# Chunk selection over 576 queries at once, with 28 products of a blank tile first and all engine lists made anew

## The chip, the cores and the metric

One Trainium2 chip, of which one core is used. The metric is device time in microseconds (us). The kernel before took 272.13 us, the median of 3 runs (272.02 to 273.0).

## The reference

Attention over 4 batches of 8 heads (768 queries and keys, 64 wide), in which each query attends to 6 chunks of 32 keys, followed by a two-layer network with an ELU between the layers. Cut to what matters:

```python
ub = np.sum(np.maximum(q[..., None, :] * k_min[...], q[..., None, :] * k_max[...]), axis=-1)
ub = np.where(causal, ub, -1e9)                    # 24 chunk bounds for each query
top_chunks = np.argsort(ub, axis=-1)[..., -6:]
scores = scale * np.matmul(q, k.transpose(0, 1, 3, 2))
mask = sel & (pos[:, None] >= pos[None, :])        # sel: the key's chunk is among top_chunks
attn = softmax(np.where(mask, scores, -1e9))
x = np.matmul(attn, v)                             # to (3072 tokens, 512)
h = x @ w_in                                       # 512 -> 2048
g = np.where(h > 0, h, np.exp(np.minimum(h, 0)) - 1)
out = g @ w_out                                    # 2048 -> 512
```

## The kernel before

**Units.** Two heads make a pair, two pairs a quad; a batch has 4 pairs and 2 quads. Queries are worked in two halves of 384 (`hf` 0 and 1). Queries below 192 (`SEL0`) have at most 6 chunks ahead of them and need no choice, so the choice covers 192 queries of the first half and 384 of the second: 576 in all.

**Preparation.** Batch 0 (`SPLIT`, pairs 0 to 3) is prepared by halves in `first_prep`: rows of k and q are loaded (L666, from SP's queue, and the first four q loads from ACT's), turned on PE by fp32 transposes, six to a tile (`turn`, L689), copied out by ACT (L699 keys, L721 queries, L725 their positive part `qa`) and reduced to chunk minima and maxima on DVE (L708, L715, tile `km`). POOL casts queries into `rhs` (L741) and values into `vext` (L732). Batches 1 to 3 (`pair_prep`) are loaded in 32 x 32 pieces (L595) and turned on DVE (L607, L625), with L611, L618, L628 and L641 as the matching steps.

**The choice.** `quad_sel(g, hf)` is called for each quad and half. On PE, 16 fp32 products (L771) make the bounds of both pairs: `km` against `qt` and `qa`, each 32 columns of output by `n/2` queries (96 for the first half, 192 for the second), in a PSUM tile of class `S2`. The profile has 32 rows for them, and 32 weight loads. DVE transposes the bounds to `ubt` (L788), writes the causal entries (L793), takes the eight largest of each group of queries to `thr` (L800, one instruction for 32 queries of each of four partition groups), compares with the sixth (L805, `selv`) and transposes back (L811, `selt`). POOL copies the result into rows 64 to 87 of `rhs` (L822, four copies a call). The scores (L863) then add the mask inside the product: `lhs` carries the chunk pattern in the same rows (L535).

**Attention.** `pair_attend(u, hf)`: scores on PE (L863, in batch 0 with the causal triangle by L869), exponentials on ACT (L890, `pt`), the triangle of batches 1 to 3 by POOL (L909), products with v (L922, `psO`), division on DVE (L935, L938), transposes on PE (L947), copies on ACT (L950, `xT`).

**The network.** `mlp(b, hf)`: `up` (L972, four products of 384 columns to a tile), the ELU on ACT (L982, L987) and DVE (L990, L1011, L1016; L1000 and L1005 in the last batch), `down` (L1032, four products of 512 columns to a part), ACT's copy to `osb` (L1041) and the store (L1046). The weights are loaded by POOL's queue (L563, L567). Work of the network of one batch fills PE while the next batch is prepared and chosen.

**Order.** Every step is an `Op` with an engine, a duration, what it reads and writes, and which buffers it takes and frees. `QUEUE` holds, for each engine, the written-out list of its steps by number; `Plan.order` walks through the five lists with the durations and a model of the loads (`ALONE`, `SHARE`, `PAUSE`) to settle in which order the program is written and which buffer each step gets. On the chip each engine then runs its own list in order and waits on semaphores. `caps` says how many buffers each class has; `kept` are tiles that are set up once (`c_kept`, `c_ones`, `c_zero`, `c_rows`).

Of the kernel before, what the change touches and what calls it, by code (L numbers as in the profile page):

```python
# [13 lines left out]
F32 = mybir.dt.float32  # L14
# [4 lines left out]
S = 768  # L19
# [7 lines left out]
P = 128  # L27
# [22 lines left out]

EARLY = (4, 0)
QUEUE = {
    "DVE": [
# [21 lines left out]
    ],  # L75
    "POOL": [
# [12 lines left out]
    ],  # L89
    "ACT": [  # L90
# [20 lines left out]
    ],  # L111
# [5 lines left out]
    ],  # L117
# [43 lines left out]
class Plan:  # L161
# [71 lines left out]
    SHARE = {128: 1.0, 256: 0.35, 512: 0.3, 768: 0.3, 1024: 0.3, 2048: 0.5}  # L233
    HEAVY = 0.088
    RAMP = 240.0
    PAUSE = ((15.8,16.6),(21.9,22.7),(29.8,30.8))
    LANDED = 0.75

    def served(self, rings, t, until):
# [875 lines left out]
```

## Time and profile before

| | before |
|---|---|
| median of 3 runs | 272.13 us |
| profiled execution | 271.44 us |
| its span, first to last instruction | 269.6 us |
| PE busy | 260.3 us (97%) |
| DVE busy | 207.2 us (77%) |
| ACT busy | 200.6 us (74%) |
| POOL busy | 122.3 us (45%) |
| bounds on PE (L771), instructions | 512 matmul rows in 16 calls |

An engine's share is of the whole span. In a timeline a row has its start, its duration, the engine, line and tiles, and in brackets how long the engine stood idle before it and what ended that. Matmuls overlap, so durations of rows on PE add up to more than PE's time; the distance from start to start is what a step costs.

### The profile page before, as it was taken

Reading aid. Unit: us, or ns where it says so; the run is one execution under the profiler, and the core shown is the slowest. Engines: PE = TensorE matmul, PEld = TensorE weight load, DVE = VectorE, ACT = ScalarE, POOL = GpSimd, SP = SyncE. Lnnn points to the kernel's source line nnn. Section 1 sums busy time; section 2 is a strip of 40 time slices with the busy share of each in tenths; the row PEclk is TensorE's granted clock in tenths of the full one; section 3 lists DMA queues with packets and bytes.
Section 4 is the critical chain, followed back from the end, with each engine's and each line's share of the span. In section 5 each row is a group of like instructions: output and inputs, shape, how many; then the busy total and the mean of one; then the engine's idle time right before and its main releaser. Section 6 shows DMA issues by size and latency. Waiting matters only on the chain.

```text
span 269.6 us, 7062 instructions
## 1 busy us (share of the span) xinstructions
PE 260.3 (97%) x2648; PEld 162.8 (60%) x2648; DVE 207.2 (77%) x562; ACT 200.6 (74%) x375; POOL 122.3 (45%) x233
## 2 busy tenths in 40 slices
PE   4998899999999999999999999999999999999995
PEld 3986566655566655655655566565666555654544
DVE  5789899899999999999898946686666785444440
ACT  4899899757996989998999386986888843234322
POOL 3697971175995798745871167434610000000000
PEclk9999999999999999999999999999999999999999
DMA  7998999989996998999621020000030100102103
GB/s 222 268 233 118 203 215 213 182 165 163 186 174 106 191 212 152 165 180 221 127 80 41 0 80 0 2 2 1 2 117 4 39 0 24 58 2 78 72 6 119
DMA packets 112626, 29.82 MB, mean 111 GB/s; under 512 B 101200, under 2 KB 109648, under 8 KB 112592
## 3 DMA queue, kind: packets, MB, share of 16 engines
q1 hardware_dynamic: 107280, 24.39, 46.0%
q0 software_dynamic: 4224, 4.19, 9.4%
q10 hardware_dynamic: 1088, 0.79, 0.9%
q8 instruction: 21, 0.34, 0.6%
q14 instruction: 13, 0.11, 0.1%
HBM read 27.26 MB, written 6.29 MB: 124 GB/s over the span
## 4 chain that ended last, share of the span: by engine, by line
PE 90%; ACT 5%; DVE 2%; DMA 1%; issue 1%; POOL 0%; ACTq 0%
PE psH L972 23%; PE psM L1032 23%; PE psS L863 13%; PE psO L922 8%; PE psS L972 8%; PE psMT L1032 8%; PE psS L771 3%; ACT lhs L699 2%; ACT pt L890 2%; PE psT L947 2%; DMA gT<-in_k_dram 1%; PE psMT L689 1%; PE psH L689 1%; PE psS L869 1%; ACT qa L725 0%
## 5 line engine op out<-in xcount | busy, mean ns | idle before, releaser
L890 ACT ACTIVATE pt<-psS 128x768 bf16<-128x768 f32 (+2 forms) x120 | 89.9, 777 | 7.7 <-PE psO L922 4.0
L972 PE MATMUL psH<-xT,w_in_sb 128*128 128x384 bf16 x384 | 75.0, 326 | 0.0
L1032 PE MATMUL psM<-w_out_sb,gT 128*128 128x512 bf16 x288 | 71.8, 379 | 0.0
L972 PEld LDWEIGHTS <-w_in_sb 128*128 128x128 bf16 x512 | 47.8, 97 | 33.0 <-issue 1.2
L1032 PEld LDWEIGHTS <-gT 128*128 128x128 bf16 x400 | 37.4, 97 | 33.6
L982 ACT ACTIVATE f<-psH 128x384 f32<-128x384 f32 x96 | 48.1, 505 | 10.8 <-PE psH L972 8.8
L863 PE MATMUL psS<-rhs,lhs 88*128 88x384 bf16 (+4 forms) x304 | 54.5, 283 | 0.7 <-ACT pt L890 0.5
L909 POOL TENSOR_SCALAR_AFFINE_SELECT pt<-pt 128x512 bf16<-128x512 bf16 (+1 forms) x48 | 24.6, 521 | 48.3 <-ACT pt L890 47.6
L1011 DVE SCALAR_TENSOR_TENSOR t<-f,psH 128x384 bf16<-128x384 f32 x56 | 30.2, 544 | 10.8 <-ACT f L982 10.0
L822 POOL COPY rhs<-selt 24x192 bf16<-24x192 bf16 (+1 forms) x64 | 27.2, 424 | 22.2 <-DVE selt L811 19.6
L863 PEld LDWEIGHTS <-lhs 88*128 88x128 bf16 x304 | 27.6, 97 | 14.6 <-ACT pt L890 1.5
L741 POOL CAST rhs<-f 64x768 bf16<-64x768 f32 (+1 forms) x40 | 28.2, 706 | 13.4 <-DVE f L625 6.5
L1016 DVE SCALAR_TENSOR_TENSOR gT<-psH,t 128x384 bf16<-128x384 f32 x56 | 30.5, 549 | 1.0
L922 PEld LDWEIGHTS <-pt 128*128 128x128 bf16 x672 | 27.2, 98 | 6.0 <-ACT pt L890 0.6
L922 PE MATMUL psO<-vext,pt 128*128 128x65 bf16 x672 | 29.7, 194 | 0.3 <-ACT pt L890 0.2
L741 POOL CAST lhs<-f 64x768 bf16<-64x768 f32 x24 | 19.7, 821 | 12.1 <-DVE f L607 11.1
L982 ACT ACTIVATE f<-psS 128x768 f32<-128x768 f32 x16 | 12.9, 811 | 16.5 <-PE psS L972 16.4
L990 DVE SCALAR_TENSOR_TENSOR gT<-f,psH 128x384 bf16<-128x384 f32 x40 | 21.6, 543 | 3.6 <-ACT psH L987 3.1
L972 PE MATMUL psS<-xT,w_in_sb 128*128 128x384 bf16 x128 | 22.9, 326 | 0.0
L1000 DVE TENSOR_SCALAR t<-f 128x768 bf16<-128x768 f32 x16 | 8.9, 558 | 17.5 <-ACT f L982 17.5
L1032 PE MATMUL psMT<-w_out_sb,gT 128*128 128x512 bf16 (+1 forms) x112 | 22.1, 349 | 0.0
L950 ACT ACTIVATE xT<-psT 128x384 bf16<-128x384 bf16 x32 | 15.4, 498 | 8.4 <-PE psT L947 8.3
(55 smaller groups left out, 299.3 us busy)
## 6 DMA issues: line engine op xcount, KB each, us to landing
out_dram<-osb SPq DMA_DIRECT2D x23, 256.0 KB, 2.3
f<-in_k_dram SPq DMA_DIRECT2D x48, 96.0 KB, 4.1
f<-in_q_dram SPq DMA_DIRECT2D x48, 96.0 KB, 3.5
f<-in_v_dram SPq DMA_DIRECT2D x24, 192.0 KB, 3.8
w_in_sb<-in_moe_w_in_dram POOLq DMA_DIRECT2D x4, 512.0 KB, 8.0
w_out_sb<-in_moe_w_out_dram POOLq DMA_DIRECT2D x4, 512.0 KB, 12.4
gT<-in_k_dram SPq DMA_DIRECT2D x8, 192.0 KB, 4.0
gT<-in_v_dram SPq DMA_DIRECT2D x12, 128.0 KB, 4.3
```

Source lines behind the costliest of these rows:

```text
L741: nc.gpsimd.tensor_copy(out=o, in_=i)
L822: eng.tensor_copy(out=dst.rearrange("c h (i two x) -> c h i two x", two=2, x=32)[:, :, :, odd, :], in_=tiles[st][r0:r0 + NCH, c0:c0 + n].r ...
L863: nc.tensor.matmul(p_s[:, hd, pc:pc + w], lhsT=tiles[pt_["kb"]][0:64 + NCH, hd, 128 * kb:128 * kb + 128], rhs=tiles[pt_["qb"]][0:64 + NCH, ...
L890: lambda bs=bs, pt=pt, wtot=wtot, lo=lo, at=at: nc.scalar.activation(out=tiles[pt][:, :, lo:lo + wtot], in_=tiles[bs[0]][:, :, at:at + wto ...
L909: nc.gpsimd.affine_select(out=a, in_=a, compare_op=AOT.is_ge, fill=0.0, base=0, pattern=pat, channel_multiplier=-1)
L922: nc.tensor.matmul(po[:, hd, qi, :], lhsT=tiles[pt][:, hd, off:off + 128], rhs=tiles[pt_["vx"]][:, 6 * hd + kb, :], start=(kb == 0), stop= ...
L972: nc.tensor.matmul(ph, lhsT=w_in_sb[:, kk, f0:f0 + 128], rhs=tiles[XT[4 * b + kk]][:, c0:c0 + HALF], start=(kk == 0), stop=(kk == NKK - 1))
L982: lambda e=e, view=view: nc.scalar.activation(out=halves(e)[:, 0:step], in_=view(), func=AF.Exp),
L990: lambda e=e, view=view, fc=fc, gt=gt: nc.vector.scalar_tensor_tensor(out=tiles[gt][:, fc:fc + step, :], in0=halves(e)[:, 0:step], scalar= ...
L1011: lambda e=e, t=t, view=view: nc.vector.scalar_tensor_tensor(out=tiles[t][:, 0:step], in0=halves(e)[:, 0:step], scalar=1.0, in1=view(), op ...
L1016: lambda t=t, view=view, fc=fc, gt=gt: nc.vector.scalar_tensor_tensor(out=tiles[gt][:, fc:fc + step, :], in0=view(), scalar=0.0, in1=tiles ...
L1032: nc.tensor.matmul(pm, lhsT=tiles[gt][:, fc, 128 * tt:128 * tt + 128], rhs=w_out_sb[:, fc, x0:x1], start=(fc == 0), stop=(fc == NFC - 1))
```

## The change

`quad_sel` gains a form for the whole row of queries: for batches 1 to 3 it is called once for each quad, with `hf=None`, and works on all 576 queries (288 columns to a product, 18 groups on DVE, transposes of 576, POOL copies of 24 x 576). Batch 0 keeps its halves. The tiles `ubt`, `thr` and `selv` grow from 12 to 18 groups, and `ubt` and `thr` have one buffer where they had two. Each call now frees the query tiles `qt` and `qa` that it read.

PE's list starts with `c_warm`: 28 bf16 products of 128 columns of a tile `blank`, which DVE fills with zeros as its first step. The result is not read.

The lists of all engines are new, with new numbers of the planner: `ALONE` 0.0188 and 0.0368 for 256 and 768 bytes, four `PAUSE` intervals, no `late` for the first loads, and other durations for the bounds on PE. Among what moves: DVE fills `ident_f` behind the five fills of `rhs`, and the copies of L535 partly behind the first reductions; POOL makes `trineg` behind the first casts; on SP the first six loads of v (L671) go ahead of the second half of k and q, of which one k load stood ahead of them.

```diff
+WARM = 28
 QUEUE = {            # all five lists replaced
...
-    ALONE = {128: 0.0138, 256: 0.0194, 512: 0.036, 768: 0.038, 1024: 0.055, 2048: 0.085}
+    ALONE = {128: 0.0138, 256: 0.0188, 512: 0.036, 768: 0.0368, 1024: 0.055, 2048: 0.085}
-    PAUSE = ((15.8,16.6),(21.9,22.7),(29.8,30.8))
+    PAUSE = ((0.0, 2.28), (17.2, 17.8), (21.6, 22.4), (30.5, 31.3))
...
-            "ubt": 2, "thr": 2, "selv": 2, "selt": 2, "pt": 10, "t": 3, "gT": 3,
+            "ubt": 1, "thr": 1, "selv": 2, "selt": 2, "pt": 10, "t": 3, "gT": 3,
...
+    blank = const.tile([P, P], BF16, name="blank")
-        "selv": [const.tile([P, 12, 32], BF16, ...
+        "selv": [const.tile([P, 18, 32], BF16, ...
-        "kx": ([P, NCH], F32), "ubt": ([P, 12, 32], F32), "thr": ([P, 12, 8], F32),
+        "kx": ([P, NCH], F32), "ubt": ([P, 18, 32], F32), "thr": ([P, 18, 8], F32),
...
+    add("DVE", 0.12, -10.5, lambda: nc.vector.memset(blank, 0.0), writes=["blank"])
     add("DVE", 0.5, -9.9, c_fill, writes=["fill"])
+    bw, = new("S2")
+
+    def c_warm():
+        for i in range(WARM):
+            nc.tensor.matmul(tiles[bw][:, 0, 0:128], lhsT=blank, rhs=blank, start=True, stop=True)
+    add("PE", 0.107 / 2 * WARM, -1000.0, c_warm, reads=["blank"], alloc=[bw], free=[bw])
...
     def quad_sel(g, hf):
         pairs = (2 * g, 2 * g + 1)
+        whole = hf is None
+        hs = (0, 1) if whole else (hf,)
+        end = whole or hf == 1
+        hf = 0 if whole else hf
...
-            n = HALF - SEL0 if hf == 0 else HALF
+            n = S - SEL0 if whole else HALF - SEL0 if hf == 0 else HALF
...
-                if hf or u in SPLIT:
-                    fr += [PAIR[u]["qt", hf], PAIR[u]["qa", hf]]
-                if hf:
+                fr += [PAIR[u]["qt", hf], PAIR[u]["qa", hf]]
+                if end:
                     fr += [PAIR[u]["km"]]
-            add("PE", 0.0025 * n + 0.073, pr, ub, reads=rd, writes=[bu[0]], alloc=bu, free=fr)
+            add("PE", 0.00167 * n + 0.27, pr, ub, reads=rd, writes=[bu[0]], alloc=bu, free=fr)
...
-                        reads=[(st, hf)], writes=[(qb, hf, odd, "left")], ...
+                        reads=[(st, x) for x in hs], writes=[(qb, x, odd, "left") for x in hs], ...
...
             for g in (2 * b, 2 * b + 1):
-                for hf in range(2):
-                    quad_sel(g, hf)
+                quad_sel(g, None)
```

More of the change, by code (lines that the diff above doesn't have):

```diff
@@ L53 @@
     "DVE": [
[21 rows of a table removed]
[20 rows of a table added]
+    ],
[32 rows of a table added]
     ],
     "POOL": [
[12 rows of a table removed]
[10 rows of a table added]
     ],
     "ACT": [
[20 rows of a table removed]
[20 rows of a table added]
     ],
     "SP": [
[4 rows of a table removed]
-    ],
[32 rows of a table removed]
[4 rows of a table added]
     ],
@@ L444 @@
         "km": [const.tile([P, 2, 32], F32, name=f"km{i}") for i in range(caps["km"])],
-        "selv": [const.tile([P, 12, 32], BF16, name=f"selv{i}") for i in range(caps["selv"])],
+        "selv": [const.tile([P, 18, 32], BF16, name=f"selv{i}") for i in range(caps["selv"])],
     }
@@ L571, in weights, with fetch @@
         add("DMA", 0.0, -20.0, lambda: None, reads=[("asked", i)], writes=[name], lat=plan.LANDED)
-    def fetch(starts, packets, size, pr, f, writes, eng="SP", more=(), late=0.0, **kw):
+    def fetch(starts, packets, size, pr, f, writes, eng="SP", more=(), **kw):
         uid[0] += 1
@@ L577, in fetch @@
         add(eng, 0.533 * starts, pr, f, reads=more, writes=[w] + writes, lat=0.0,
-            move=(0 if eng == "SP" else 1, (1.08 if eng == "SP" else 1.3) + late, 0.533, starts, packets, size), **kw)
+            move=(0 if eng == "SP" else 1, 1.08 if eng == "SP" else 1.3, 0.533, starts, packets, size), **kw)
         add("DMA", 0.0, pr, lambda: None, reads=[w], writes=writes, lat=plan.LANDED)
@@ L674, in first_prep @@
         early = u - SPLIT[0] < EARLY[hf]
-        late = 0.35 if u == SPLIT[0] and hf == 0 else 0.0
-        fetch(1, 256, 768, pl, load(i0, kr), [(sg, i0)], late=late, alloc=[sg] if u == SPLIT[0] else [])
+        fetch(1, 256, 768, pl, load(i0, kr), [(sg, i0)], alloc=[sg] if u == SPLIT[0] else [])
         fetch(1, 256, 768, (pl + 0.1) - 300.0 * early, load(i0 + 1, qr, nc.scalar if early else nc.sync), [(sg, i0 + 1)],
-              eng="ACT" if early else "SP", late=late)
+              eng="ACT" if early else "SP")
         if u % 2 == 0:
@@ L776, in quad_sel @@
             for u in pairs:
-                rd += [PAIR[u]["qt", hf], PAIR[u]["qa", hf], (PAIR[u]["km"], 0, hf), (PAIR[u]["km"], 1, hf)]
-                if hf or u in SPLIT:
-                    fr += [PAIR[u]["qt", hf], PAIR[u]["qa", hf]]
-                if hf:
+                rd += [PAIR[u]["qt", hf], PAIR[u]["qa", hf]] + [(PAIR[u]["km"], i, x) for i in range(2) for x in hs]
+                fr += [PAIR[u]["qt", hf], PAIR[u]["qa", hf]]
+                if end:
                     fr += [PAIR[u]["km"]]
-            add("PE", 0.0025 * n + 0.073, pr, ub, reads=rd, writes=[bu[0]], alloc=bu, free=fr)
+            add("PE", 0.00167 * n + 0.27, pr, ub, reads=rd, writes=[bu[0]], alloc=bu, free=fr)
             ut, = new("ubt")
@@ L812, in t2 @@
                                     in_=tiles[sv].rearrange("p a b -> p (a b)")[:, 0:n])
-            add("DVE", dve(n), pr, t2, reads=[sv], writes=[(st, hf)], alloc=[] if hf else [st], free=[sv])
+            add("DVE", dve(n), pr, t2, reads=[sv], writes=[(st, x) for x in hs], alloc=[] if hf else [st], free=[sv])
             for j, u in enumerate(pairs):
@@ L826, in quad_sel @@
                     add("DVE" if fast else "POOL", 0.075 + 0.00027 * n if fast else 0.20 + 0.00095 * n, pr + 0.01, put,
-                        reads=[(st, hf)], writes=[(qb, hf, odd, "left")], free=[st] if hf and j and odd else [],
+                        reads=[(st, x) for x in hs], writes=[(qb, x, odd, "left") for x in hs],
+                        free=[st] if end and j and odd else [],
                         port=True)
```

175 rows, old and new, of the table QUEUE are left out of this document.

## The prediction

> **What bounds the kernel now.** I read the page first, then PE's waits over the whole span and from 32 us on, then the busy time of each engine by stage, and last the timelines of the first 11 us and of one selection. The page's first part and its chain:
>
> ```profile
> PE 260.3 (97%) x2648; PEld 162.8 (60%) x2648; DVE 207.2 (77%) x562; ACT 200.6 (74%) x375; POOL 122.3 (45%) x233
> ...
> PE 90%; ACT 5%; DVE 2%; DMA 1%; issue 1%; POOL 0%; ACTq 0%
> ```
>
> PE carries nine tenths of the chain that ended last. A busy PE is no proof by itself, since matmuls overlap, so I asked what PE waited for (us in total, times, longest):
>
> ```profile
> PE psH L689 <- DMA gT<-in_k_dram: 4.0, 1, 4.0
> PE psT L947 <- DVE on L938: 0.9, 2, 0.6
> ```
>
> And the same from 32 us to the end, the whole answer but its first two lines:
>
> ```profile
> PE psO L922 <- ACT pt L890: 0.2, 1, 0.2
> ```
>
> So the run has two parts. Behind 32 us PE has work at every moment: 0.2 us of waits in 238 us. There a microsecond of PE work removed is a microsecond of time, and what DVE, ACT or POOL save is worth nothing until it ends a wait. Ahead of 32 us PE waits, first for the keys (4.0 us), then here and there for others. By stage:
>
> ```profile
> core 0: us, PE busy (x) PEld busy (x) DVE busy (x) ACT busy (x) POOL busy (x), PEclk, DMA share, GB/s
> ...
> 4.00:8.00 4.00, 3.96 (x19) 3.62 (x20) 2.93 (x11) 2.70 (x6) 0.58 (x1) 1.00 1.11 328
> ...
> 12.00:16.00 4.00, 4.00 (x73) 3.79 (x72) 3.33 (x17) 3.92 (x12) 3.77 (x9) 1.00 1.20 288
> ...
> 60.00:80.00 20.00, 19.99 (x193) 11.70 (x185) 19.91 (x51) 17.74 (x33) 15.76 (x29) 1.00 1.06 176
> 80.00:100.00 20.00, 20.00 (x255) 12.04 (x240) 19.88 (x57) 15.94 (x29) 15.02 (x29) 1.00 0.95 169
> ```
>
> From 12 us ACT works 3.92 of 4 us: the start belongs to ACT, and only in 4 to 8 us (2.70 of 4) is it kept waiting. DVE is full from 60 to 100 us (39.8 of 40), so a list that leans on DVE there has no room.
>
> **The bounds of batches 1 to 3.** One quad of pairs, first half and then second half, with a piece of other work on each side (timeline of PE; start, duration):
>
> ```profile
> 57.21 0.81 PE L972 MATMUL psH<-xT,w_in_sb 128*128 128x384 bf16 x4
> 57.95 0.40 PE L771 MATMUL psS<-f,km 64*32 64x96 f32 x16
> ...
> 58.44 1.04 PE L1032 MATMUL psM<-w_out_sb,gT 128*128 128x512 bf16 x4
> 59.41 0.56 PE L771 MATMUL psS<-f,km 64*32 64x192 f32 x16
> ...
> 60.22 0.66 PE L972 MATMUL psH<-xT,w_in_sb 128*128 128x384 bf16 x3
> ```
>
> Eight L972 products run in 1.30 us and four L1032 products in 0.86 us, as the chain in order of time has them, with one of the two quads whose halves lie side by side:
>
> ```profile
> 75.44 1.30 PE psH L972 x8
> ...
> 79.89 1.28 PE psS L771 x64
> ...
> 85.25 1.73 PE psM L1032 x8
> ```
>
> The four L972 products end at 57.21 + 0.65 = 57.86, and PE is free for others at 58.44: the 96-column half takes 0.58. The L1032 products end at 58.44 + 0.86 = 59.30, and the next work starts at 60.22: the 192-column half takes 0.92. Side by side the two take 1.28 and about 0.1 of entry, 1.38. A step of 96 columns costs 0.34, so one set of 288 columns is an estimate of 0.92 + 0.34 = 1.26. Of the six quads four are apart (1.50 to 1.26, 0.24 each) and two side by side (0.12 each): 1.2 us off PE. Bounds: in pure proportion to columns 288 would cost 1.5 x 0.92 = 1.38, which leaves 0.5; if of the fixed part of a set (0.58 - 0.34 = 0.24) only the 0.1 of entry stayed, 3 x 0.34 + 0.1 = 1.12, which gives 2.0. I take 1.2, as both rows lie on that line, and all of it is behind 32 us, so all of it is time.
>
> On DVE and POOL the same edit merges two instructions into one:
>
> ```profile
> L811 DVE STREAM_TRANSPOSE selt<-selv 128x384 bf16<-128x384 bf16 x8 | 4.5, 564 | 0.1
> L822 POOL COPY rhs<-selt 24x192 bf16<-24x192 bf16 x32 | 11.1, 348 | 19.3 <-DVE selt L811 18.0
> ...
> L805 DVE TENSOR_TENSOR selv<-ubt,thr 128x288 bf16<-128x288 f32 x8 | 3.6, 454 | 0.1
> L822 POOL COPY rhs<-selt 24x384 bf16<-24x384 bf16 x32 | 16.0, 501 | 2.9 <-DVE selt L811 1.6
> ...
> L805 DVE TENSOR_TENSOR selv<-ubt,thr 128x144 bf16<-128x144 f32 x8 | 2.5, 309 | 0.1
> L811 DVE STREAM_TRANSPOSE selt<-selv 128x192 bf16<-128x192 bf16 x8 | 2.9, 362 | 0.1
> ```
>
> By these lines the whole-row transpose is 0.77 (0.93 before, in two), the comparison 0.60 (0.76), the POOL copy 0.65 (0.85). With two transposes a quad saves about 0.5 us of DVE and 4 x 0.2 = 0.8 of POOL: 3 and 5 us in all, priced at nothing since neither engine makes PE wait there.
>
> What is added is a longer way from bounds to scores: no score beyond query 192 of the first half starts before the choice for the second half is made too. On DVE: transpose 0.77, 18 maxima, comparison 0.60, transpose 0.77; twelve maxima take
>
> ```profile
> 30.57 1.04 DVE L800 MAX8 thr<-ubt 128x8 f32<-128x14 f32 x12
> ```
>
> so 18 take 1.56: 3.7 us, and then two to four POOL copies, 1.3 or 2.6. PE's new list puts 7.6, 5.8 and 8.7 us of other work (L972 and L1032 products at the durations above, a few scores) between the bounds of the first three quads and the first score that reads them, and over 12 for the last three. Against 6.3, 5.0 and 6.3 us of chain, plus other DVE steps in between (0.5, 0.9 and 1.5 us by the list), the room is 0.8, nearly nothing, 0.9. I take 0.1 us of new waits.
>
> The single ubt and thr buffers cost nothing by themselves: DVE is the only engine that touches them, in its own order.
>
> **The blank products.** PE's first steps, six transposes to a tile:
>
> ```profile
> 4.04 1.51 PE L689 MATMUL psH<-ident_f,gT 128*128 128x128 f32 x6 [4.04 <-DMA gT<-in_k_dram]
> 5.35 2.76 PE L689 MATMUL psMT<-ident_f,gT 128*128 128x128 f32 x12
> 7.91 1.66 PE L689 MATMUL psH<-ident_f,gT 128*128 128x128 f32 x12
> 9.41 0.82 PE L689 MATMUL psMT<-ident_f,gT 128*128 128x128 f32 x6
> 10.06 0.82 PE L689 MATMUL psH<-ident_f,gT 128*128 128x128 f32 x6
> ```
>
> Six take 1.31 at first (5.35 - 4.04) and 0.65 later (10.06 - 9.41): half clock, then full. Twelve from 7.91 take 1.50, so about two of them were still slow: the clock rose near 8.3, 4.2 us behind PE's first work. The 28 products come as soon as DVE has written the blank tile. In the trace before DVE and POOL began so:
>
> ```profile
> 0.90 0.17 DVE L499 MEMSET ident_f<- 128x128 f32 x1 [0.90 <-PEq L1099]
> ...
> 1.30 1.05 DVE L530 MEMSET rhs<- 32x192 uint32 x5
> ...
> 2.19 0.29 POOL L507 TENSOR_SCALAR_AFFINE_SELECT ident_f<-ident_f 128x128 f32<-128x128 f32 x1
> ```
>
> A blank tile written first is there at 1.1, and PE starts at about 1.2. At twice the 54 ns that 128 columns take at full clock (four L1032 products, 2048 columns, take 0.86) the products last 3.0 us, to about 4.3, which puts the first real transpose off by 0.3. That ident_f is now filled behind the five fills of rhs (1.05 later, and POOL has wider selv tiles to clear ahead of it) costs nothing: at some 0.5 to 1 us past 2.48 it is still there before 4.04; uncovered it would be that much. The clock then rises at 1.2 + 4.2 = 5.4 at the latest, and the slow stretch of real work falls from 4.2 us (2.1 lost) to 1.1 (0.55 lost): PE is 2.1 - 0.55 - 0.3 = 1.25 us ahead at 10 us.
>
> [...]
>
> What of this reaches the end? ACT is next:
>
> ```profile
> 5.59 0.98 ACT L699 ACTIVATE lhs<-psH 64x384 bf16<-64x384 f32 x2 [0.56 <-PE psH L689]
> 6.87 0.49 ACT L721 ACTIVATE f<-psMT 128x384 f32<-128x384 f32 x1 [0.30 <-PE psMT L689]
> ...
> 8.15 0.49 ACT L721 ACTIVATE f<-psMT 128x384 f32<-128x384 f32 x1 [0.57 <-PE psMT L689]
> ```
>
> The last two gaps, 0.87, close; the first stays, since the first tile is ready no earlier. After that ACT has had no gaps to close, so 0.9 is the ceiling from this cause, and the loads take some back. SP's list:
>
> ```profile
> 0.81 3.77 SPq L666 DMA_DIRECT2D gT<-in_k_dram  x5
> 4.63 4.17 SPq L671 DMA_DIRECT2D gT<-in_v_dram  x6
> ```
>
> Before, the fifth load (first keys of the second half) leaves ahead of six loads of v; now it stands behind them, so it leaves near 8.3 instead of 4.2. The 16 loads of L666 land
>
> ```profile
> DMA to landing us min/median/max: 3.1/4.1/5.4
> ```
>
> after issue: at 12.4 (11.4 to 13.7). PE's new list comes to it after eight tiles, one score tile and the first bounds, 6.2 us of work: 4.3 + 0.55 + 6.2 = 11.1. ACT has 17 steps ahead of it; at some 0.4 us each (the first row has two in 0.98, and 2.70 us for six stand in the 4 to 8 us row) it wants the result at 5.6 + 6.8 = 12.4, and with the middle landing gets it at 12.4 + 0.65 + 0.2 = 13.2. The early landing costs nothing, the late one all of the gain; I let 0.3 of the 0.9 go: 0.6 stays.
>
> The lists made anew also change the small waits ahead of 32 us (0.9 for DVE in two pieces): from 0.9 better to as much worse. I take 0.3 better, since blank tile, casts and maxima now start earlier on all three engines.
>
> **Sum.** The profiled execution took 271.44 us, span 269.6 and 1.84 around it, and the median of the three runs, 272.13, lies 0.7 above it. 271.44 - 1.2 - 0.6 - 0.3 + 0.1 = 269.4; with the 0.7, 270.1 for the median.
>
> **Rivals.** *The start gives nothing*: the blank products raise the clock no earlier, or the late keys take all of it back. For it: ACT at 3.92 of 4, the six loads put ahead. Against: 0.87 of gaps that plainly end at slow transposes. 272.1 - 1.2 = 270.9 (271.2 with the 0.3 of delay). Chance 0.18.
>
> *All of it reaches the end*: bounds at 2.0, PE's lead of 1.25 in full, and the 0.9 of DVE waits gone: 272.1 - 4.15 = 268.0. Against it stands ACT. Chance 0.12 for 267.6 to 269.0.
>
> *Scores wait for the choice*, the case on the slow side. Place: PE's first score of the first three quads, with 0.8, nothing and 0.9 us of room. PE keeps its order, so each microsecond by which DVE comes later than that is idle PE. DVE is full from 60 to 100 us, its L811 steps come behind whatever the list queues ahead, and POOL's copies behind them. It decides from about 0.6 us of lateness; at 2 us in each of three quads it costs 3 x 2 - 1.7 = 4.3, so 274.4. Against: DVE has 0.5 us less to do in each quad. Chance 0.18 for 273.5 and more.
>
> [...] The rows of PE's first steps speak against it; chance 0.02. [...]
>
> **How the numbers follow.** The forecast, 269.0 to 270.8, has 0.50. Of the first rival a quarter falls below 270.77. About half a per cent, 1.4 us, is what a measurement of this kernel tells from no change. Faster by more: 0.50 + 0.12 + 0.04 = 0.66; within: 0.14 + 0.02 = 0.16; slower: 0.18. The range from 267.7 to 273.0 leaves out most of the slow case and little else.
>
> **What would show it.** Right: one set of bounds per quad at 1.2 to 1.3 us of PE; transposes at 0.65 for six by 5.4; ACT's gaps at 6.9 and 8.2 gone; the first L972 product near 31.4, which before stood at
>
> ```profile
> 32.33 1.46 PE L972 MATMUL psH<-xT,w_in_sb 128*128 128x384 bf16 x8
> ```
>
> and PE waits behind it under 1 us. Wrong: PE waiting for L822 copies at 65, 85 or 105 us; a wait of the turn tiles for in_k_dram of over 1 us near 12; six transposes still at 1.3 behind 6 us.

## The result, and the profile after

The kernel after took 276.32 us (median of 6 runs, 274.26 to 277.94), the kernel before beside it 272.56 us (6 runs): a ratio of 1.0154, 95% interval 1.0123 to 1.0186. It is slower, by 3.8 us of median. Its profiled execution took 274.26 us (span 272.6), 2.8 us over the 271.44 us of before, and was the fastest of its six: four of them show a mean granted clock of 0.992 to 0.994, the profiled one 1.0. That matters below. Ratios leave out the few executions marked as slow, among them one of e3's six, at 691 us.

The page's busy times and its chain, to be held against the first two lines shown of before:

```profile
PE 261.4 (96%) x2484; PEld 162.3 (60%) x2484; DVE 206.7 (76%) x533; ACT 201.0 (74%) x375; POOL 118.6 (44%) x209
...
PE 73%; DMA 9%; ACT 6%; DVE 5%; SPq 4%; issue 1%; ACTq 0%; POOL 0%; DVEq 0%
```

PE still carries most of the chain, but 73% and not 90%: DMA, ACT and SP's queue (SPq) have come into it. PE's waits (us in total, times, longest), in the order of the whole answer:

```profile
PE psH L694 <- DMA gT<-in_k_dram: 1.5, 3, 1.0
PE psH L981 <- ACT osb L1050: 1.3, 1, 1.3
PE psS L542 <- DVE blank L536: 1.1, 1, 1.1
PE psH L981 <- DMA w_in_sb<-in_moe_w_in_dram: 0.8, 1, 0.8
PE psT L956 <- DVE on L947: 0.7, 1, 0.7
PE psS L878 <- POOL trineg L502: 0.5, 1, 0.5
```

The 4.0 us for the first keys are gone from the list since PE is busy with blank products (L542) by then. In their place stand 1.5 us for keys in three pieces. And behind 32 us, where before had 0.2 us of waits in all, there are now 1.3 us for `osb` and 0.8 us for w_in. The 0.7 us for `on` end at 32.01 and belong to the start, where before waited 0.9 us for `on`.

The first product of the network, where before stood 32.33, and PE's next products from the second w_in transfer:

```profile
33.55 1.46 PE L981 MATMUL psH<-xT,w_in_sb 128*128 128x384 bf16 x8
...
36.55 0.82 PE L981 MATMUL psH<-xT,w_in_sb 128*128 128x384 bf16 x4 [0.76 <-DMA w_in_sb<-in_moe_w_in_dram]
```

So the start lost 1.2 us where I forecast a gain of 0.9. From this product to PE's last one passed 234.0 us before and 235.7 us after. As the bounds take 1.4 us less (below), that stretch has lost 3.1 us elsewhere. The waits that the profile lists in it grew by 2.1 us; the other 1.0 us is taken up below, under "The longer choice".

### The profile page after: what moved, and what is told of

Same layout as the page of the kernel before. It is cut to its first block, busy times and chain, and to the rows that moved or that the text cites. A ratio compares the mean times of both kernels' runs of the same rounds, so it can differ in the third digit from the quotient of the medians.

```text
span 272.6 us, 6657 instructions
## 1 busy us (share of the span) xinstructions
PE 261.4 (96%) x2484; PEld 162.3 (60%) x2484; DVE 206.7 (76%) x533; ACT 201.0 (74%) x375; POOL 118.6 (44%) x209
## 4 chain that ended last, share of the span: by engine, by line
PE 73%; DMA 9%; ACT 6%; DVE 5%; SPq 4%; issue 1%; ACTq 0%; POOL 0%; DVEq 0%
PE psM L1041 19%; PE psH L981 19%; PE psS L872 9%; PE psS L981 8%; PE psMT L1041 8%; PE psO L931 6%; ACT pt L899 4%; DMA w_in_sb<-in_moe_w_in_dram 3%; DMA out_dram<-osb 2%; DMA gT<-in_q_dram 2%; PE psS L780 2%; DMA gT<-in_k_dram 2%; SPq L601 2%; PE psT L956 1%; SPq L677 1%
## 5 line engine op out<-in xcount | busy, mean ns | idle before, releaser
L872 PE MATMUL psS<-rhs,lhs 88*128 88x384 bf16 (+4 forms) x304 | 55.2, 283 | 0.7 <-ACT pt L899 0.4
L918 POOL TENSOR_SCALAR_AFFINE_SELECT pt<-pt 128x256 bf16<-128x256 bf16 (+1 forms) x48 | 24.4, 521 | 66.4 <-ACT pt L899 54.3
L991 ACT ACTIVATE f<-psH 128x384 f32<-128x384 f32 x96 | 47.0, 497 | 8.5 <-PE psH L981 6.9
L872 PEld LDWEIGHTS <-lhs 88*128 88x128 bf16 x304 | 27.5, 98 | 16.0 <-issue 2.8
L830 POOL COPY rhs<-selt 24x576 bf16<-24x576 bf16 (+2 forms) x40 | 22.7, 567 | 19.4 <-DVE selt L819 15.9
L959 ACT ACTIVATE xT<-psT 128x384 bf16<-128x384 bf16 x32 | 15.5, 494 | 10.2 <-PE psT L956 10.2
L1041 PE MATMUL psMT<-w_out_sb,gT 128*128 128x512 bf16 (+1 forms) x112 | 22.7, 349 | 0.0
L996 ACT ACTIVATE psH<-psH 128x384 f32<-128x384 f32 x40 | 19.8, 504 | 0.0
```

Of the source, the lines that this page charges most:

```text
L830: eng.tensor_copy(out=dst.rearrange("c h (i two x) -> c h i two x", two=2, x=32)[:, :, :, odd, :], in_=tiles[st][r0:r0 + NCH, c0:c0 + n].r ...
L872: nc.tensor.matmul(p_s[:, hd, pc:pc + w], lhsT=tiles[pt_["kb"]][0:64 + NCH, hd, 128 * kb:128 * kb + 128], rhs=tiles[pt_["qb"]][0:64 + NCH, ...
L918: nc.gpsimd.affine_select(out=a, in_=a, compare_op=AOT.is_ge, fill=0.0, base=0, pattern=pat, channel_multiplier=-1)
L991: lambda e=e, view=view: nc.scalar.activation(out=halves(e)[:, 0:step], in_=view(), func=AF.Exp),
L1041: nc.tensor.matmul(pm, lhsT=tiles[gt][:, fc, 128 * tt:128 * tt + 128], rhs=w_out_sb[:, fc, x0:x1], start=(fc == 0), stop=(fc == NFC - 1))
```

## Experiments

All times are medians of device time, and each ratio stands against runs of the kernel before on the same chip. Three questions: what the blank products do, what the order of the start does, and where the late loss comes from.

**e1: the blank products alone.**

```diff
 # kernel before, its choice by halves, its lists
+DVE:  memset(blank)        # first step
+PE:   c_warm               # first step, 28 products of 128 columns
```

> The kernel before, all its lists and its choice by halves kept; only the 28 blank products and the fill of their tile are put ahead of PE's and DVE's lists. Theory L (the new lists lost the time, the blank products are harmless or help a little): 271.5 to 272.5 us, about 0.6 under the kernel before, the first up product at 31.7 instead of 32.3 us. Theory W (the blank products themselves do harm, by delaying the first loads or an instruction fetch): slower than the kernel before by 1 us or more, first up product at 33 or later.

272.53 us against 271.99: 1.0027 (1.0008 to 1.0047), and the first up product stood at 33.22. Theory W's direction, if not its full size. The transposes did run faster early: twelve from 5.64 us take 1.32, where in the kernel before twelve from 5.35 take 2.56. But PE, now ahead, meets the keys of the second half:

```profile
15.83 0.84 PE L698 MATMUL psH<-ident_f,gT 128*128 128x128 f32 x6 [1.16 <-DMA gT<-in_k_dram]
```

They land some 1.3 us later than in the kernel before. Something in the loads differs, as the DMA view from 12 to 14 us has it, first of the kernel before, then of e1 (a queue's packets, MB, share of 16 engines):

```profile
DMA packets 901, 0.65 MB, mean 327 GB/s; under 512 B 50, under 2 KB 901, under 8 KB 901
...
q1 hardware_dynamic: 901, 0.65, 108.6%
```

```profile
DMA packets 725, 0.54 MB, mean 269 GB/s; under 512 B 46, under 2 KB 724, under 8 KB 724
...
q1 hardware_dynamic: 724, 0.52, 92.2%
q8 instruction: 1, 0.02, 3.1%
```

One packet of instructions (16 KB, q8) stands among the loads of e1 and not among those of before, and the loads moved 0.52 MB instead of 0.65 in these 2 us. The DMA records put its start at 12.57 us in e1 and at 17.07 us in before, behind the keys.

That this packet makes the keys late is not shown, and part of the delay is older than it. SP asks for these three key loads from 10.62 us on in e1 and from 9.92 in before, 0.7 us later; from there to landing they take 4.5 to 4.7 us instead of 3.9 to 4.1, and at most these 0.6 us can be the packet's. Two traces of later runs speak against more: e9, with no such packet before 17.46 us, asks for the same loads as late (10.55) and moves 0.58 MB from 12 to 14 us, and e10, with one at 13.60, moves 0.64 MB and waits for no key. Why SP asks later in e1 is open.

**e2: the kernel after without the blank products.**

```diff
 # kernel after, its merged choice, its lists
-DVE:  memset(blank)
-PE:   c_warm
```

> The kernel after, all its lists and its merged choice kept; only the 28 blank products and the fill of their tile are taken out. Theory L: the start stays late because the loads' order stays, 276 to 277.5 us, first up product at 33.5 or later. Theory W: 1 us or more is won, 275 us or less.

1.0179 (1.0152 to 1.0205), 276.67 us, first up product at 33.47: theory L's figures. The interval overlaps that of the kernel after, so on the new lists the blank products neither pay nor cost anything that can be measured, and they are not the cause of the loss.

**e3 and e4: the two starts exchanged.**

```diff
 # e3: kernel after                       # e4: e1
-first ~31 us: after's order             -first ~30 us: before's order
+first ~31 us: before's order            +first ~30 us: after's order
```

> The kernel after with its merged choice and blank products; on every engine the steps that the kernel before starts in its first 31 us stand first, in the order of the kernel before, and all other steps follow in the order of the kernel after. Theory L: the 1.4 us lost ahead of the first up product and the 0.9 us lost to the later w_in transfers come back, 273.5 to 274.2 us, first up product at 32.3 or earlier; about 1.4 us around the store wait at 111 us stays. Theory S (the merged choice makes scores and later steps late): the start comes back, but the loss reappears later, 275.5 us or more.

> The kernel before with its choice by halves, and the blank products; on every engine the steps that the kernel after starts in its first 30 us stand first, in the order of the kernel after, and the rest follow in the order of the kernel before. Theory L: the start loses what it loses in the kernel after, 274 to 275 us, first up product at 33.3 to 33.7. Theory S: the order of the start costs nothing, 271.9 to 272.7 us.

e3 gave 1.0175 (1.0131 to 1.0219): theory L fell. With the old start the first up product stood at 33.68, w_in was waited for no less, and the late loss was there in full. e4 gave 1.0059 (1.0036 to 1.0082), 273.32 us: near 0.8 us over e1, with intervals that overlap. So the start, blank products and order together, is the smaller part (1.3 us), and the larger sits behind 32 us. Theory S was not confirmed by that, since e3's trace pointed elsewhere: PE waited 2.0 us for `osb` near 112 us, and then (busy times and granted clock by stage, windows of 4 us)

```profile
core 0: us, PE busy (x) PEld busy (x) DVE busy (x) ACT busy (x) POOL busy (x), PEclk, DMA share, GB/s
...
110.00:114.00 4.00, 2.24 (x14) 1.25 (x14) 3.32 (x6) 1.96 (x5) 3.25 (x6) 1.00 1.14 238
114.00:118.00 4.00, 3.67 (x23) 2.29 (x23) 2.11 (x4) 2.70 (x7) 3.60 (x7) 0.63 1.22 196
118.00:122.00 4.00, 4.00 (x56) 2.52 (x61) 2.14 (x6) 3.79 (x8) 2.29 (x3) 0.95 1.11 118
```

PE was busy for 2.24 of 4 us, and the next stretch ran at a granted clock of 0.63: (0.37 + 0.05) x 4 = 1.7 us of PE's time (six L872 products from 116.65 take 1.26 us, in the kernel after the six from 113.27 take 0.66). The profiled execution of e2 has the same: a wait of 1.95 us for `osb` up to 113.33, then a granted clock of 0.59 from 114 to 118. Four of the six runs of the kernel after have a mean clock that is lower by as much (0.6% of 272 us is 1.6 us), so the wait for `osb` is probably paid twice in them, by an estimate from the mean clock alone; where in these runs the clock fell is not on record, and the profiled one did not lose it (granted 1.00 from 110 to 122 us).

**Where `osb` comes from.** In the kernel after, ACT's copies of the network's output, of which three buffers exist:

```profile
61.69 0.60 ACT L1050 ACTIVATE osb<-psM 128x512 f32<-128x512 f32 x1 [1.61 <-PE psM L1041]
66.33 0.60 ACT L1050 ACTIVATE osb<-psM 128x512 f32<-128x512 f32 x1 [0.95 <-PE psM L1041]
77.60 0.66 ACT L1050 ACTIVATE osb<-psM 128x512 f32<-128x512 f32 x1
92.83 0.60 ACT L1050 ACTIVATE osb<-psM 128x512 f32<-128x512 f32 x1 [0.22 <-DMA out_dram<-osb]
102.35 0.62 ACT L1050 ACTIVATE osb<-psM 128x512 f32<-128x512 f32 x1
111.07 0.60 ACT L1050 ACTIVATE osb<-psM 128x512 f32<-128x512 f32 x1 [1.28 <-DMA out_dram<-osb]
```

and SP's queue ahead of the last of them, with PE behind it:

```profile
99.51 6.82 SPq L601 DMA_DIRECT2D f<-in_q_dram  x8
106.43 1.06 SPq L643 DMA_DIRECT2D f<-in_v_dram  x2
107.59 0.49 SPq L1055 DMA_DIRECT2D out_dram<-osb  x1
108.19 2.79 SPq L601 DMA_DIRECT2D f<-in_k_dram  x4
111.02 0.80 SPq L1055 DMA_DIRECT2D out_dram<-osb  x1
...
111.72 1.46 PE L981 MATMUL psH<-xT,w_in_sb 128*128 128x384 bf16 x8 [1.27 <-ACT osb L1050]
```

By the lists, the store of the copy at 61.69 is the one issued at 111.02, and that of 66.33 comes after it. Two of three buffers hold finished results for 45 us and more, so every copy from 92.83 on has one buffer, and that one is free only when the store, queued behind loads, has landed (issued 107.59, landed 110.99 by the DMA records, copy at 111.07). ACT keeps its order, so the ELU's steps and PE stand behind that copy. The list before left the second copy's store as late (122.39 us), but asked for the first copy's ahead of all others, and so kept two buffers in use:

```profile
86.75 0.53 SPq L1046 DMA_DIRECT2D out_dram<-osb  x1
```

**e6: one store earlier.**

```diff
 "SP": [
-  ... 917, 966, 430, 980, 951, ... 506, 1317, 418, 1351,
+  ... 917, 966, 418, 430, 980, 951, ... 506, 1317, 1351,
```

> The kernel after; one change in SyncE's list: the store of the first 128 rows of the first half, whose result lies in its buffer from 62 us on and whose store was asked for at 111.0 us behind the loads of pairs 11, 12 and 14, is asked for ahead of the store that the kernel after asks for first, at about 89 us. Theory Q (the late loss is ScalarE's copies waiting for an output buffer whose store stands in SyncE's list behind loads): the wait of 1.3 us at 111 us goes, and with it the clock window at half speed that most runs have behind it (1.7 us): 273.2 to 275.0 us. Rival S (the merged choice makes scores and copies late by itself): 275.8 us or more, PE waits as long elsewhere between 90 and 115 us.

273.1 us, 1.0029 (1.0003 to 1.0054): 3.2 us of 3.8 came back, each against its own runs of the kernel before, from one number moved in one list. The same copy no longer waits, two stores are asked for together at 88.83, and PE's waits from 32 us on are down to 0.8 us in all:

```profile
109.00 0.60 ACT L1050 ACTIVATE osb<-psM 128x512 f32<-128x512 f32 x1
...
88.83 1.09 SPq L1055 DMA_DIRECT2D out_dram<-osb  x2
...
PE psH L981 <- DMA w_in_sb<-in_moe_w_in_dram: 0.4, 1, 0.4
PE psH L981 <- ACT xT L959: 0.2, 1, 0.2
PE psS L872 <- ACT pt L899: 0.2, 1, 0.2
```

One of its 12 runs has a clock of 0.994, the rest 0.998 and over. Theory Q stands. Between the two profiled executions, both at a mean granted clock of 1.0, lie only 1.9 us, of which the start gives 0.5 and w_in 0.4; so the wait itself is 1.0 to 1.3 us of the 3.2. The rest, I argue, is the low clock of the other executions.

**e7: the bounds products split again, nothing else.**

```diff
-for w in range(2): ...                      # 576 queries
+for cut in ((0, 192), (192, 576)):
+    for w in range(2): ...
```

> The kernel after, all lists kept; the bounds products of a quad in batches 1 to 3 are done in the same step but as two column sets (192 and 384 queries) as in the kernel before; everything behind them stays merged. Theory P (the merged products take 1.4 us off PE and PE passes it on): 277.3 to 278.0 us, a set pair 0.23 us longer than 1.23 us. Rival H (PE has waits elsewhere that would absorb it): within 0.5 us of the kernel after, 275.8 to 276.8 us.

277.98 us, 1.0206 (1.0172 to 1.0239), 1.7 us over the kernel after: theory P's figure, but the interval touches that of the kernel after, so it is not settled that PE's work here is not absorbed. On PE:

```profile
59.17 0.81 PE L982 MATMUL psH<-xT,w_in_sb 128*128 128x384 bf16 x4
59.92 0.40 PE L781 MATMUL psS<-f,km 64*32 64x96 f32 x16
60.11 0.37 PE L781 MATMUL psS<-qa,km 64*32 64x96 f32 x16
60.27 0.64 PE L781 MATMUL psS<-f,km 64*32 64x192 f32 x16
60.60 0.64 PE L781 MATMUL psS<-qa,km 64*32 64x192 f32 x16
61.17 1.04 PE L1042 MATMUL psM<-w_out_sb,gT 128*128 128x512 bf16 x4
```

From 59.17 + 0.65 = 59.82 to 61.17 is 1.35 for the two side by side, 0.12 over the merged set (below) and not the 0.23 I had expected; 0.7 us for six quads. The rest of the 1.7 us is within the interval; its profiled run also waited 2.5 us for `osb` where the kernel after waited 1.3, with a mean granted clock of 1.0.

**e5: the same blank time with fewer instructions.**

```diff
 # e1
-c_warm: 28 products of 128 columns
+c_warm:  7 products of 512 columns
```

> The kernel before with 7 blank products of 512 columns ahead of PE's work instead of 28 of 128 columns: about the same 3 us of PE's time with 14 instructions instead of 56. In the runs with 28 products the first 16 KB fetch of instructions began at 12.5 to 14.3 us, among the loads of the second-half k, and at 17.07 us in the kernel before, behind them. Theory F (the blank products cost because their instructions pull that fetch forward into the loads): the fetch begins at about 16 us, the wait of 1.3 us ahead of the second-half k goes, first up product at 31.7 to 32.3 us, 271.5 to 272.0 us. Rival E (an early full clock only makes PE arrive sooner at loads that land at the same time, or the products themselves slow the first loads): the wait stays, first up product at 33.0 or later, 272.5 us or more.

1.0002 (0.9976 to 1.0028), first up product at 32.91, instruction fetch at 13.78: between the two theories, and the interval overlaps that of e1. Inconclusive on the number of instructions. The wait for the keys was gone although the fetch came early, which theory F had tied together. But with 14 added instructions the fetch still came 3.3 us earlier than before. That would fit PE being ahead as the cause, more than the blank products' own instructions, but no run separates the two.

**e8 and e9: old start, merged choice, early stores.**

```diff
 # kernel after, without blank products
-first ~42 us: after's order
+first ~42 us: before's order
 # SP, e8: the store of e6;  e9: every store of batches 0 and 1 that stood behind loads, moved ahead
```

> Merged choice, no blank products; every engine's list has first the steps that the kernel before starts in its first 42 us, in its order, then the rest in the order of the kernel after, and the one store asked for early as in e6. Theory L+Q (order of the start, blank products and the store are the whole loss, the merge a gain of 1.4 us): 270.4 to 271.4 us, faster than the kernel before. Rival S: 272.5 us or more with waits of PE between 58 and 115 us.

> As e8 (merged choice, no blank products, the first 42 us in the order of the kernel before), but every store of batches 0 and 1 that stood behind loads in SyncE's list is asked for about 3 us behind the copy that fills its buffer: the first half's three at about 63, 69 and 80 us, the second half's third at 111 us. In e8 ScalarE waited 1.6 us at 92.7 us for the one store moved there, and PE 1.3 us behind it. Theory Q: both waits go, 272.0 to 272.6 us, at or just under the kernel before: the merge's 1.4 us is then nearly eaten by 0.6 us of w_in and some 0.7 us of small waits. Theory L+Q in full (nothing else was lost): 270.8 to 271.5 us. Rival D (the stores push the loads of pairs 8 to 15 late, which PE then waits for): 273.5 us or more.

e8 missed: 273.78 us, 1.0069 (1.0037 to 1.0101). The wait had moved one copy ahead, as the store moved there still came too late by 1.6 us:

```profile
92.72 0.60 ACT L1041 ACTIVATE osb<-psM 128x512 f32<-128x512 f32 x1 [1.59 <-DMA out_dram<-osb]
```

e9, with the first three stores at 65, 73 and 84 us (4 to 7 us behind their copies), gave 272.29 us, 0.9987 (0.9969 to 1.0005): what theory Q had given, level with the kernel before.

**e10, e11 and e12: what is left.**

```diff
 # e10: e9 + 7 blank products of 512 columns
 # e11: e9, POOL:
-  put, put, w_in[1]
+  w_in[1], put, put
 # e12: e11 + 7 blank products of 512 columns
```

> As e9, with 7 blank products of 512 columns ahead of PE's work. Theory E (the start is bound by the loads, an early clock brings nothing): within 0.5 us of e9, more likely above it. Theory of the prediction (an early clock keeps 0.6 us): 0.4 to 0.8 us under e9.

> As e9, and on GpSimd the second of the w_in transfers is asked for ahead of the two copies of the choice that it stood behind (at about 26.1 instead of 27.9 us). In e9 PE waited 1.13 us for it at 36.1 us. If that wait is the largest part still lost: it goes, 271.0 to 271.7 us, under the kernel before. If the transfers only crowd each other (the landing stays at 35 to 36 us) or the copies come late for PE: 272.0 to 272.8 us as e9.

> As e11, with 7 blank products of 512 columns ahead of PE's work (as e10). If an early clock is worth nothing because the loads set the start: within 0.4 us of e11. If it is worth what the prediction kept, 0.6 us: 0.4 to 0.8 us under e11.

0.9989 (0.9968 to 1.0010), 0.9986 (0.9960 to 1.0012) and 0.9989 (0.9960 to 1.0017). The blank products brought nothing that can be measured in either pair. In e11's trace the wait for w_in is gone, and the time did not follow by more than the interval. All three are about 4 us under the kernel after; none is shown to beat the kernel before.

The starts of all kernels in one table, one profiled execution each (first up product, start of the first instruction fetch by the DMA records, us):

| order of the start | without blank products | with |
|---|---|---|
| before's | before 32.33 / 17.07; e8 32.41 / 15.48; e9 32.73 / 17.46; e11 32.58 / 17.44 | e1 33.22 / 12.57; e3 33.68 / 12.51; e5 32.91 / 13.78; e10 32.42 / 13.60; e12 34.35 / 14.12 |
| after's | e2 33.47 / 14.89 | after 33.55 / 14.34; e4 33.46 / 13.59; e6 33.02 / 13.84; e7 34.02 / 14.72 |

With before's order and no blank products the fetch comes at 15.5 us or later and the first up product at 32.3 to 32.7. Otherwise the fetch comes at 12.5 to 14.9, and the product anywhere from 32.4 to 34.4.

## Why the prediction was wrong, point by point

The step that failed most is "the lists made anew": priced at 0.3 us of gain, looked for only ahead of 32 us, with the stores at nothing. It cost about 0.8 us there and 3.2 us behind, through one store. Next comes the 0.6 us that the blank products were to keep, and did not.

**What bounds the kernel.** Right in the main. Behind the first up product e6's profiled execution has 1.5 us less of PE waits than the kernel after, and is 1.4 us shorter there; e7, with more PE work, points the same way. What I did not draw from it is the reverse. A list with 0.2 us of waits in 238 us has no cover for any new wait, and the new lists put new ones there.

**Bounds of batches 1 to 3.** Right as PE's time; what of it reached the end is a question for the longer choice, below. The kernel after, PE's timeline around the same quad:

```profile
58.74 0.81 PE L981 MATMUL psH<-xT,w_in_sb 128*128 128x384 bf16 x4
59.48 0.71 PE L780 MATMUL psS<-f,km 64*32 64x288 f32 x16
59.99 0.69 PE L780 MATMUL psS<-qa,km 64*32 64x288 f32 x16
60.61 1.04 PE L1041 MATMUL psM<-w_out_sb,gT 128*128 128x512 bf16 x4
```

58.74 + 0.65 = 59.39 to 60.61: 1.22 for a set of 288 columns, against an estimate of 1.26. Worked out so for all six quads, PE's time goes from 8.77 to 7.36 us: 1.4 us against the 1.2 forecast.

**The blank products.** What the prediction calls the clock here is the pace of PE's products, 1.31 and later 0.65 us for six transposes; the granted clock in the traces reads 1.00 in every window of 1 us from 0 to 10 us, before and after. Right in direction: the faster pace came earlier than before's 8.3. In the profiled execution of the kernel after the second tile's six transposes already start 0.65 ahead of the third's.

```profile
4.02 1.08 PE L694 MATMUL psH<-ident_f,gT 128*128 128x128 f32 x6
4.94 0.82 PE L694 MATMUL psMT<-ident_f,gT 128*128 128x128 f32 x6
5.59 0.82 PE L694 MATMUL psH<-ident_f,gT 128*128 128x128 f32 x6
```

The faster pace came by 4.94, ahead of my 5.4, but that was luck. In e1 the first tile, from 4.38 to 5.64, was slow throughout, and in e7, whose blank products start at the same 1.06 us, both of the first two tiles are slow, 1.28 each:

```profile
4.02 1.49 PE L694 MATMUL psH<-ident_f,gT 128*128 128x128 f32 x6
5.30 1.49 PE L694 MATMUL psMT<-ident_f,gT 128*128 128x128 f32 x6
6.58 1.63 PE L694 MATMUL psH<-ident_f,gT 128*128 128x128 f32 x12
8.04 0.82 PE L694 MATMUL psMT<-ident_f,gT 128*128 128x128 f32 x6
```

Twelve from 6.58 take 1.46, so the rise there is an estimate of 6.9. My "5.4 at the latest" was wrong: counted from the start of the same 28 products, the faster pace was there within 3.9 us in one execution and 5.8 in another. What sets that time is not shown.

The 0.02 in the sum of chances was for a pace that falls again behind the blank products. No run shows that: in the kernel before nothing but transposes ran ahead of 8.3 us, and their pace rose near there; in the kernel after nothing but transposes ran from 4.02 to 11.4 us, and every tile of six from 4.94 on lasted 0.82 to 0.88 us, where the first of before lasted 1.51.

What failed is the step "what of this reaches the end": 0.6 us kept, from "ACT is next" and "0.9 is the ceiling, and the loads take some back". I priced the loads with their landing times of before, as if these were fixed. They are not: in e1 the keys that PE waited for landed some 1.3 us later than before, and the start then hangs on the loads and no longer on ACT. What delays them is not shown; the earlier instruction fetch is one candidate, for half of it at most (e1, above). By stage, e1, in which nothing but the blank products was added:

```profile
12.00:16.00 4.00, 2.52 (x30) 2.31 (x29) 3.60 (x17) 3.15 (x8) 3.77 (x9) 1.00 1.04 272
16.00:20.00 4.00, 3.89 (x72) 3.48 (x71) 1.33 (x10) 3.25 (x10) 2.71 (x8) 1.00 1.07 235
```

ACT, at 3.92 of 4 us from 12 us before, is down to 3.15 and 3.25. The step measured, by itself, +0.5 us (e1) and not −0.6; in the other pairs (e2 and the kernel after, e9 and e10, e11 and e12) it was worth nothing that can be measured.

**The late keys.** I named a wait of over 1 us for in_k near 12 us as the sign against me. It came as three waits, the longest of 0.98 us at 18.6 us: a tile later in the list, behind the fetch at 14.34; whether that fetch or the place of the load in SP's list made it late was not separated.

**The lists made anew.** This term was mis-sized and looked for in the wrong place: I gave it 0.3 us of gain, and only ahead of 32 us. There the new order cost about 0.8 us (e4 against e1, intervals overlapping), some of it from `trineg` on POOL, which PE waited 0.5 us for. Behind 32 us I priced only PE's list against the choice and never read SP's list past the first loads. One store placed behind loads of pairs 8 to 14 cost 3.2 us (e6).

**The longer choice.** The 0.1 us of new waits was of the right kind: PE waits nowhere on a copy of the choice by POOL (L830) behind 32 us, and the two it has for `xT` and `pt` in e6 are of 0.2 us each. But not all of the merge's gain arrives. In e11, from the first up product to PE's last, 233.9 us pass against 234.0 before, although the bounds take 1.4 us less; the listed waits grew by 0.4 us, and 0.9 us is in none of them. Worked out in the same way, with 1.7 us for the low clock of e2 and e3, nine of the ten profiled executions with a merged choice leave 0.8 to 1.2 us without a name. The exception is e12, with e11's lists behind the start: 233.1 us, and nothing left over. So in the nine only about 0.4 us of the merge's 1.4 arrived net of this, where I had taken 0.1 us of new waits. Whether the longer way from bounds to scores or the order of the lists makes this loss was not separated: the old lists with a merged choice in them were not tried. Added up, −1.4 for the bounds, +0.5 for the blank products, +0.8 for the order of the start, +3.2 for the store and this +1.0 make +4.1 us, against 3.8 measured; the store's term alone is uncertain by about 1 us.

**Rivals.** The slow side had 0.18, at 274.4 us, by "scores wait for the choice". The sign was right, the mechanism not: no score waited for a choice. "The start gives nothing" happened as well, which by its own working would have given 270.9. No rival had a store.

## What to carry to other kernels

When all lists are made anew, read each queue's list to its end, stores and loads alike: for each buffer class, find when its last reader is queued, and what stands in front of it. Here a store queued behind loads (issued 107.59, landed 110.99) held a buffer, the buffer held ACT's copy for 1.28 us, and that copy held PE for 1.27. A gain at the start counts only once the next resource in line is priced as it will be when everything upstream arrives earlier, with the spread of its loads from one execution to the next.

## What the hardware showed that I had not expected

A wait of 2.0 us on PE was followed by a loss of another 1.7 us through the clock (granted 0.63 over 4 us in e3; 0.59 in e2, behind a wait of 1.95), so in these two executions the stall was paid almost twice. Others differ: a mean clock of 0.994 or less stands in four of six runs of the kernel after and in one of twelve of e6, and e7's profiled execution waited 2.5 us at the same place and kept a mean clock of 1.0, so the length of the wait alone did not decide it. What does is not shown: 0.992 to 0.994 stands also in four of twelve runs of e12, whose profiled execution waits for no `osb`.

A 16 KB instruction fetch took 0.9 to 1.7 us in these traces. That it holds up the loads beside it is not shown: in e12 PE waited 2.05 us for keys at 16.8 us, behind a fetch at 14.12, and in e10, with a fetch at 13.60, for none. The first one began at 12.5 to 14.7 us in every kernel with blank products and at 15.5 to 17.5 us in those with the old order and without them (14.89 in e2, with the new order and without them). That PE's progress sets it is argued from these times, not shown by itself.
